# When the decays' maxima and the verdict's ones are issued in a fused decay-attention and gated-MLP kernel

## The chip, the cores and the metric

The kernel runs on one core of one Trainium2 chip. The metric is the device time in microseconds of one execution. A profiled execution gives a span (first to last recorded instruction) and a trace of every engine: TensorE (PE, with its weight loads as PEld), VectorE (DVE), ScalarE (ACT), GpSimd (POOL) and SyncE (SP), which issues all the DMAs here.

## The reference, cut to what matters

```
for t in range(S):                       # S = 768, 4 batches x 8 heads, D = 40
    y[:, :, t] = r_t @ state
    Sa = state @ a_t
    state = state * w_t - outer(Sa, b_t) + outer(v_t, k_t)
x = y as [batch, 768, 320]
h = gelu(x @ w_in)                       # 320 -> 1024; u, v are its halves
v_n = (v - mean) / sqrt(var + 1e-6) * g_ln
v_s = einsum('ts,bsd->btd', w_sg, v_n) + b_sg
out = x + (u * v_s) @ w_out
```

The decays `w` (named `seq_w` in the kernel) are inputs, so the kernel also has to find out whether its chunked form of the recurrence is safe for them. It takes the maximum of the absolute decays and compares it with 1, and it compares the chunks' products of decays with a least value. If either fails, a plain step-by-step version runs instead.

## The kernel before, in words

The **first part** (`attention`) runs the recurrence in chunks of 64 steps and writes x to DRAM. The first weights of the MLP, the first batch's x and three of its v products are worked into its last stretch. The **second part** (`Mlp.run`, line 980 and on) is a list `seq` of 109 products, numbered from 0, each of which is a group of 8 to 18 matmuls into one PSUM bank:

- `v` (one 128-row tile of v, 8 matmuls of 512 columns), followed on ACT, DVE and POOL by gelu, batch statistics, normalising and a split into a high and a low part, `vh` and `vl`;
- `u` (8 matmuls of 384 columns), followed by gelu;
- `s` (the product along the sequence, 18 matmuls of 384 columns that read `vh` and `vl` of all six v tiles), followed by two DVE operations into `g`, then `gy` on ACT and `gx` on POOL;
- `o` (the output product, 8 or 12 matmuls that read `gy` and `gx`), followed by the residual sum `y` on DVE and a store.

Products 0 to 10 finish u and v of batch 0. Then come 28 products for each of the batches 0, 1 and 2 (11 to 38, 39 to 66, 67 to 94) in the order `SEQ`: s1 s2 s0 s3 s4 v0 s5 v1 o0 o1 o2 s6 s7 v2 u0 v3 u1 v4 v5 o3 o5 o4 u2 u3 u4 u5 u7 u6, where s and o belong to the batch, u and v to the next one. The last 14 are s and o of batch 3. The PSUM banks are taken in turn, eight of them.

Every engine works its own queue in program order (class `InOrder`). Program order comes from two tables. A **job** is a pair (product number, function) and is issued just before that product; of jobs with one number, the one entered first goes first. What follows a product is given to `later` as (lag, rank, function). `tick`, called after each product's matmuls, issues whatever is due, sorted by rank. So a step of lag 2 is issued after the matmuls of the product two further on.

What the change and the prediction's steps touch:

- `GROWTH = 12` (line 31) is the product number of the first of 20 jobs `growth(j)`, entered for the products 12 to 31. `growth` takes one of the five buffers `ws` (which first held pieces of the sequence weights), issues a 192 KB DMA of decays on SP, and enters with lag 2 and rank 8 one DVE reduction of 128 x 384 to a column of `wm`. So the reductions come behind the products 14 to 33.
- Before the s products of the next batch, jobs load x: `load_x(b + 1, n)` for both halves n (eight DMAs on SP) at the batch's first product (11, 39, 67), `split_x` one product later (ACT copies to `xh`, DVE writes `xl`). The v products of the next batch read these.
- `verdict` (line 584) is called as a job at the product 73. It compares `wm` and the decays' products with their limits and reduces each to one column of `fl`. Its inner function `last` is entered with lag 8 and rank 9, so it is issued behind u0, the product 81. `last` clears the column `ends` to ones on DVE, multiplies it with `fl` on TensorE into a bank `fp`, and makes the flag from that on DVE.
- Ahead of `last` in that same tick stand, by rank, DVE operations that the products v2 (80) and u0 (81) entered: gelu's steps (rank 6 and 6.5), `bn_stats` (7) and `bn_aggr` (8) of v2.

```
jobs += [(GROWTH + j, lambda j=j: self.growth(j)) for j in range(20)]
jobs.append((p + 6, lambda: self.later((8, 9, verdict(self.wm)))))
```

The DVE queue therefore holds, behind v2 and u0: gelu of both, the statistics of v2, the clearing of `ends`, and then the flag's operations. TensorE's queue holds: v2, u0, the two passes of `fp`, v3.

Of the kernel before, what the change touches and what calls it, by code (L numbers as in the profile page):

```python
# [9 lines left out]
F32 = mybir.dt.float32  # L10
# [17 lines left out]
GROWTH_MAX = 1.0  # L28
DECAY_MIN = 1e-08
DECAY_LOW = 1e-09  # L30
GROWTH = 12
HI_MIN = float(np.uint32(896 << 20).view(np.float32))
HI_MAX = float(np.uint32(1151 << 20).view(np.float32))
FIRST = 0
# [85 lines left out]
def engines(tc):  # L120
    nc = tc.nc
    return tuple(InOrder(tc, e) for e in (nc.vector, nc.scalar, nc.gpsimd, nc.tensor, nc.sync))
# [6 lines left out]
def attention(tc, a, xd, flag, keep, ps, mlp=None):  # L129
# [3 lines left out]
    V, A, G, T, Q = engines(tc)  # L133
# [450 lines left out]
    def verdict(wm):  # L584

        cf = call.rearrange("p i q -> p (i q)")
        fl = keep.tile([128, 2], F32, name="fl")
        V.tensor_scalar(out=wm, in0=wm, scalar1=GROWTH_MAX, scalar2=None, op0=ALU.is_le)
        V.tensor_scalar(out=cf, in0=cf, scalar1=DECAY_MIN, scalar2=None, op0=ALU.is_ge)
        V.tensor_reduce(out=fl[:, 0:1], in_=wm, axis=mybir.AxisListType.X, op=ALU.min)  # L590
        V.tensor_reduce(out=fl[:, 1:2], in_=cf, axis=mybir.AxisListType.X, op=ALU.min)

        def last():
            ends = keep.tile([128, 1], F32, name="ends")
            V.memset(ends, 1.0)
            fp = ps("fp")
            T.matmul(fp[0:1, 0:2], lhsT=ends, rhs=fl, start=True, stop=True)
            V.tensor_reduce(out=fl[0:1, 0:1], in_=fp[0:1, 0:2], axis=mybir.AxisListType.X, op=ALU.add)
            V.tensor_scalar(out=flag, in0=fl[0:1, 0:1], scalar1=255.5, scalar2=None, op0=ALU.is_lt)

        return last
# [4 lines left out]
class Mlp:  # L606
# [323 lines left out]
    def run(self, ahead, verdict=None):  # L930
# [18 lines left out]
        for b in range(B):  # L949
# [5 lines left out]
            if b == 2 and verdict:  # L955
                jobs += [(GROWTH + j, lambda j=j: self.growth(j)) for j in range(20)]
                jobs.append((p + 6, lambda: self.later((8, 9, verdict(self.wm)))))
# [133 lines left out]
```

## Time and profile before

| | before |
|---|---|
| time, median of 3 runs | 670.6 us (669.77 to 670.92) |
| the profiled execution's own time | 667.9 us |
| its span | 666.2 us |
| PE busy | 580.6 us (87% of the span) |
| DVE busy | 519.8 us (78%) |
| ACT busy | 369.8 us (56%) |
| POOL busy | 385.3 us (58%) |
| mean granted clock of TensorE | 0.899 of full speed |

The profiled execution lies 1.7 us above its own span and 2.7 us below the median of the runs. In the trace an instruction has a start and a length; an idle time in square brackets is that of its engine just before it, with what ended it. All the recorded operations carry one line (L115, the helper that keeps program order), so they are told apart by the names of their tiles. The granted clock is 1.00 at 2.4 GHz and 0.50 at 1.2 GHz.

### The profile page before, as it was taken

How to read it: one execution, taken by the hardware profiler on the slowest of the kernel's cores; microseconds unless marked ns; L12 is line 12 of the kernel's file. 1: busy time of each engine (PE TensorE's matmuls, PEld its weight loads, DVE VectorE, ACT ScalarE, POOL GpSimd, SP SyncE). 2: the span in 40 equal slices, each digit the busy share in tenths (PEclk: the TensorE clock that was granted, in tenths of full speed). 3: DMA queues.
4: the chain of work that ended last, by engine and by line, in shares of the span. 5: the costliest groups of instructions: out<-in, count | busy, mean ns of one | idle time of the engine just before them, and what ended most of it. 6: DMA issues, size and time to landing. Idle time of an engine off the chain costs nothing.

```text
span 666.2 us, 22344 instructions
## 1 busy us (share of the span) xinstructions
PE 580.6 (87%) x8950; PEld 526.7 (79%) x8950; DVE 519.8 (78%) x1118; ACT 369.8 (56%) x1010; POOL 385.3 (58%) x868
## 2 busy tenths in 40 slices
PE   6547999989989899899979864969999999989995
PEld 5436788878878788787878754959999999979994
DVE  7875788989889899897786688887898669666732
ACT  3454587876968769687755644652345245223410
POOL 6588887787877878778872464453332332332321
PEclk8555599999999999999967695969999999999999
DMA  6723233444434534333435240451422003000001
GB/s 222 231 80 79 80 94 107 117 120 107 110 102 115 122 109 108 103 89 94 104 94 145 81 130 22 126 156 49 125 66 84 31 0 102 1 30 13 19 30 37
DMA packets 60498, 60.49 MB, mean 91 GB/s; under 512 B 36256, under 2 KB 50336, under 8 KB 60384
## 3 DMA queue, kind: packets, MB, share of 16 engines
q1 hardware_dynamic: 60384, 58.96, 31.4%
q8 instruction: 73, 1.20, 0.8%
q14 instruction: 41, 0.34, 0.2%
HBM read 51.07 MB, written 7.86 MB: 88 GB/s over the span
## 4 chain that ended last, share of the span: by engine, by line
PE 54%; DVE 25%; ACT 12%; issue 6%; DMA 3%; POOL 1%; SPq 0%; POOLq 0%; DVEq 0%; ACTq 0%
PE sg L115 15%; PE hu L115 7%; PE op L115 6%; PE hv L115 6%; PE ru L115 4%; PE ab L115 4%; DVE at L115 3%; PE pq L115 3%; DVE fixed L115 3%; DVE n L115 2%; PE sp L115 2%; PE yp L115 2%; DVE ex L115 2%; ACT xt L115 2%; ACT nts L115 2%
## 5 line engine op out<-in xcount | busy, mean ns | idle before, releaser
L115 POOL TENSOR_TENSOR tg<-x,n 128x126 f32<-128x126 f32 (+21 forms) x348 | 127.9, 368 | 42.8 <-DVE n L115 10.5
L115 POOL TENSOR_TENSOR x<-x,tg 128x126 f32<-128x126 f32 (+21 forms) x348 | 133.4, 383 | 27.3
L115 POOL TENSOR_TENSOR gx<-g,gy 128x384 fp32r<-128x384 f32 x32 | 33.3, 1045 | 84.9 <-ACT gy L115 84.9
L115 PE MATMUL sg<-wsh,vh 128*128 128x384 f32 x192 | 66.4, 346 | 5.0 <-ACT vh L115 5.0
L115 ACT ACTIVATE nts<-ab 32x256 f32<-32x256 f32 x192 | 62.0, 323 | 11.0 <-DVE at L115 8.6
L115 PE MATMUL sg<-wsh,vl 128*128 128x384 f32 x192 | 66.1, 344 | 1.5 <-POOL vl L115 1.5
L115 PE MATMUL yp<-pqs,kbt 128*64 128x64 f32 x768 | 49.9, 236 | 18.9 <-DVE pqs L115 15.4
L115 PE MATMUL sg<-wsl,vh 128*128 128x384 f32 x192 | 65.8, 343 | 0.0
L115 PE MATMUL ab<-at,kb 64*64 64x64 f32 x1536 | 41.9, 248 | 25.7 <-DVE kb L115 18.9
L115 PEld LDWEIGHTS ab<-at,kb 64*64 64x64 f32 x1536 | 35.1, 155 | 33.7 <-issue 18.3
L115 PE MATMUL pq<-rt,vut 128*128 128x128 f32 x384 | 59.8, 304 | 1.7 <-DVE yt L115 1.6
L115 PEld LDWEIGHTS yp<-pqs,kbt 128*64 128x64 f32 x768 | 40.5, 147 | 22.1 <-DVE pqs L115 16.0
L115 ACT CAST gy<-g 128x384 fp32r<-128x384 f32 x32 | 16.4, 513 | 74.3 <-DVE g L115 74.3
L115 PEld LDWEIGHTS pq<-rt,vut 128*128 128x128 f32 x384 | 51.6, 208 | 4.8 <-DVE yt L115 2.5
L115 ACT COPY vs<-sc 64x160 f32<-64x160 f32 x88 | 28.3, 321 | 44.0 <-DVE sc L115 43.1
L115 POOL TENSOR_TENSOR vl<-v,vh 128x512 fp32r<-128x512 f32 x24 | 31.3, 1305 | 26.6 <-ACT vh L115 26.6
L115 ACT CAST vh<-v 128x512 fp32r<-128x512 f32 x24 | 14.9, 620 | 57.2 <-DVE v L115 57.2
L115 PE MATMUL yp<-rt,s 80*40 80x64 f32 x704 | 46.2, 232 | 0.0
L115 DVE SCALAR_TENSOR_TENSOR g<-sg,gl,bt 128x384 f32<-128x384 f32 x32 | 19.7, 615 | 30.0 <-PE sg L115 28.1
L115 POOL TENSOR_TENSOR rs<-rs,mhalf 128x1 f32<-128x1 f32 x24 | 13.4, 560 | 50.6 <-DVE rs L115 43.7
L115 PEld LDWEIGHTS sg<-wsh,vh 128*128 128x128 f32 x192 | 36.8, 192 | 5.8 <-ACT vh L115 5.7
L115 DVE TENSOR_TENSOR at<-ab,mask 64x256 f32<-64x256 f32 x96 | 35.8, 408 | 6.1 <-PE ab L115 5.4
(134 smaller groups left out, 1639.3 us busy)
## 6 DMA issues: line engine op xcount, KB each, us to landing
main<-main SPq DMA_DIRECT2D x88, 160.8 KB
vu<-vs SPq DMA_DIRECT2D x24, 160.0 KB
vs<-vb SPq DMA_DIRECT2D x24, 160.0 KB
rt<-rt SPq DMA_DIRECT2D x48, 80.0 KB
vut<-vt SPq DMA_DIRECT2D x24, 160.0 KB
xd<-yt SPq DMA_DIRECT2D x96, 40.0 KB
ws<-seq_w SPq DMA_DIRECT2D x20, 192.0 KB
xt<-xd SPq DMA_DIRECT2D x16, 192.0 KB
```

Of the source, the lines that this page charges most:

```text
L115: return self.tc.keep_in_program_order(f(*a, **k))
```

## The change

The 20 jobs `growth` begin at the product 34, so their loads are issued ahead of the products 34 to 53 and their reductions behind the products 36 to 55. The tile `ends` is taken and cleared at the head of `verdict`, at the product 73, instead of in `last`.

```diff
-GROWTH = 12
+GROWTH = 34
...
         fl = keep.tile([128, 2], F32, name="fl")
+        ends = keep.tile([128, 1], F32, name="ends")
+        V.memset(ends, 1.0)
         V.tensor_scalar(out=wm, in0=wm, scalar1=GROWTH_MAX, scalar2=None, op0=ALU.is_le)
         V.tensor_scalar(out=cf, in0=cf, scalar1=DECAY_MIN, scalar2=None, op0=ALU.is_ge)
         V.tensor_reduce(out=fl[:, 0:1], in_=wm, axis=mybir.AxisListType.X, op=ALU.min)
         V.tensor_reduce(out=fl[:, 1:2], in_=cf, axis=mybir.AxisListType.X, op=ALU.min)
 
         def last():
-            ends = keep.tile([128, 1], F32, name="ends")
-            V.memset(ends, 1.0)
             fp = ps("fp")
             T.matmul(fp[0:1, 0:2], lhsT=ends, rhs=fl, start=True, stop=True)
```

## Rows read from the trace of the kernel before

**Rows 1.** The page, its part 2: granted clock in 40 slices of 16.7 us.

```profile
PEclk8555599999999999999967695969999999999999
```

**Rows 2.** Waits of PE, 413 to 666 us: total us, times, longest.

```profile
PE sg L115 <- ACT vh L115: 5.0, 2, 3.8
PE fp L115 <- DVE ends L115: 2.8, 1, 2.8
PE sg L115 <- POOL vl L115: 1.5, 2, 1.1
PE op L115 <- ACT gy L115: 0.8, 1, 0.8
PE op L115 <- POOL gx L115: 0.5, 1, 0.5
```

**Rows 3.** Timeline: an s product's last wait; then 592 to 600 us.

```profile
441.95 0.69 PE L115 MATMUL sg<-wsh,vl 128*128 128x384 f32 x1 [0.34 <-POOL vl L115]
...
592.87 0.86 PE L115 MATMUL hv<-wih,xh 128*128 128x512 f32 x3
...
595.77 0.51 PE L115 MATMUL hu<-xl,wih 128*128 128x384 f32 x2
...
598.87 0.18 DVE L115 BATCH_NORM_AGGREGATE mv<-bs 128x2 f32<-128x6 f32 x1
599.00 0.06 DVE L115 MEMSET ends<- 128x1 f32 x1
...
599.11 0.19 PE L115 MATMUL fp<-fl,ends 128*1 128x2 f32 x2 [2.83 <-DVE ends L115]
...
599.23 1.47 PE L115 MATMUL hv<-wih,xh 128*128 128x512 f32 x3
```

**Rows 4.** Stretches around the wait: us, PE, PEld, DVE, ACT, POOL busy, clock, DMA.

```profile
598.00:600.00 2.00, 0.89 (x4) 0.72 (x5) 1.33 (x7) 0.00 (x0) 0.20 (x1) 0.87 0.00 0
600.00:602.00 2.00, 2.00 (x6) 1.56 (x5) 0.00 (x0) 0.00 (x0) 0.35 (x1) 0.50 0.00 0
```

**Rows 5.** Timeline, PE: v2, v3, then s1, batch 1; s1 of batch 3.

```profile
534.16 0.86 PE L115 MATMUL hv<-wih,xh 128*128 128x512 f32 x3
...
537.40 0.86 PE L115 MATMUL hv<-wih,xh 128*128 128x512 f32 x3
...
558.26 0.34 PE L115 MATMUL sg<-wsh,vh 128*128 128x384 f32 x1
...
621.74 0.34 PE L115 MATMUL sg<-wsh,vh 128*128 128x384 f32 x1
```

**Rows 6.** Timeline, DVE, 576.5 to 579 us: the verdict's last reduction.

```profile
577.79 0.35 DVE L115 TENSOR_REDUCE fl<-call 128x1 f32<-128x192 f32 x1
```

**Rows 7.** Tile ws: ns min/median/max, first and last start.

```profile
L115 SPq DMA_DIRECT2D ws<-seq_w x20: 327/346/572, 444.4 to 493.7; - x20
L115 DVE TENSOR_REDUCE wm<-ws x20: 534/542/548, 455.7 to 499.8; 128x1 f32<-128x384 f32 x20
```

**Rows 8.** Timeline, DVE: y of o4 in batch 0, g of s1, end of split_x; y of o4, batch 1.

```profile
498.43 0.54 DVE L115 TENSOR_TENSOR y<-op,xt 128x384 f32<-128x384 f32 x1
...
504.92 0.60 DVE L115 SCALAR_TENSOR_TENSOR g<-sg,gl,bt 128x384 f32<-128x384 f32 x1
...
510.32 0.56 DVE L115 TENSOR_TENSOR xh<-xt,xh 64x384 fp32r<-64x384 f32 x1
...
555.26 0.54 DVE L115 TENSOR_TENSOR y<-op,xt 128x384 f32<-128x384 f32 x1
```

**Rows 9.** Timeline, PE: s1 (39) and v0 (44) behind the loads of batch 2's x.

```profile
499.55 0.34 PE L115 MATMUL sg<-wsh,vh 128*128 128x384 f32 x1
...
515.39 0.86 PE L115 MATMUL hv<-wih,xh 128*128 128x512 f32 x3
```

**Rows 10.** Timeline, SP: the issues of batch 2's x.

```profile
499.39 4.38 SPq L115 DMA_DIRECT2D xt<-xd  x8
```

**Rows 11.** A stretch of batch 1's loads: us, DVE busy, clock, DMA share, GB/s.

```profile
443.00:445.00 2.00, 1.97 (x5) 0.50 0.85 250
```

## The prediction, made before the change was run

> **What bounds the kernel now.** I began with the clock by slices. Its last low digit is the slice from 433 to 450 us, behind the start of the second part at about 413 us; from there on it is 9 in every slice [rows 1]. A slice of 16.7 us can hide a short stop, so the next view was the waits of PE from 413 us to the end. There are only five kinds: two for the splits of v, four waits of which the last ends at 441.95 us [rows 3]; two for `gy` and `gx` of the last products; and between them one single wait of 2.8 us, of `fp` for `ends` [rows 2]. So the second part is bound by TensorE, and another engine's work matters there only if it makes TensorE wait. The timeline around that wait shows why. u0's last matmuls end at 595.77 + 0.51 = 596.28 us. DVE then still works on gelu of v2 and u0 and on the statistics of v2, and clears `ends` only at 599.00 us, behind `bn_stats` and `bn_aggr`. `fp` runs at 599.11 us after 2.83 us of idling, and v3, which needs nothing of the verdict, stands behind it until 599.23 us [rows 3]. After that the granted clock is 0.50, that is 1.2 GHz, through 600 to 602 us, and the mean of the two microseconds before is 0.87: it fell after the idle stretch [rows 4].
>
> **Part 1, the ones.** What `fp` still needs after the change is `fl`, and its last reduction begins at 577.79 us and takes 0.35 us [rows 6]: 18 us early. The ones are cleared just before that. So TensorE goes from u0 through `fp` to v3 at once. The price of the wait can be read against a control: batch 1 runs the same order of products without a verdict. From the start of v2 to the start of s1 of the next batch takes
>
> - batch 1: 558.26 - 534.16 = 24.10 us, and batch 2: 621.74 - 592.87 = 28.87 us, a difference of 4.77 us [rows 3, 5];
> - of these, v2 to v3: 3.24 against 6.36 us, so 3.12 us lie in the idle stretch and `fp` itself;
> - and v3 to s1: 20.86 against 22.51 us, so 1.65 us are matmuls at half the clock.
>
> The two passes of `fp` stay: from 599.11 to 599.23 us, 0.12 us. The gain is 4.77 - 0.12 = **4.65 us**, of which 3.0 us are the wait and 1.65 us the clock. The clearing of 0.06 us [rows 3] moves to the product 73 on a DVE that TensorE does not wait for there; if that cover were gone it would cost those 0.06 us and no more. What is late next: v3, u1, v4, v5 come 3 us earlier on DVE's queue, which had idled meanwhile. In batch 1 the same products follow u0 without a gap and PE waits for none of them [rows 2, 5], so I set nothing against it. The flag itself is read by the branch behind the last product, long after.
>
> Here one thing is not sure. The row shows the clock falling after this idle stretch in this one execution. The Trainium skill, in "TensorE: Matmul & The Clock Gate" (Part 1: The HAM clock gate), says that the monitor runs freely and does not restart with the kernel, so that the point of a change of clock differs between runs of one kernel. By the trace the sum is 4.65 us; by that rule some executions of the kernel before would not lose the 1.65 us, and the sum would be 3.0 us. No row here shows an execution of that kind.
>
> **Part 2, the maxima.** Twenty reductions of 0.54 us, 10.8 us of DVE, leave the stretch from 455.7 to 499.8 us [rows 7], and twenty DMA issues of 0.35 us leave SP there. PE does not wait between 442 us and `fp` [rows 2, 3], so taking them away there gains nothing. They come back behind the products 36 to 55, some 500 to 544 us.
>
> What they could cost there lies between nothing and 10.8 us, if all of it lay on TensorE's path. I take nothing. Behind the products 25 to 33 (u0, the v products, the o products and u2 of batch 0's stretch, where DVE has most to do) nine of them stood, and PE waited for none. After the change that heavy passage of batch 1 holds only four of them (52 to 55) and batch 0's none. In between, the reductions behind 36 to 43 meet the u products and `split_x` of batch 2. Up to the product 55 DVE has always done fewer of them than before, so by the sum of its work it is nowhere later in this stretch than it was; one s product after another then gives it slack. Below nothing I see no room: a gain needs a wait that is not there.
>
> SP is the other queue. The first five loads are now issued ahead of batch 2's x, where before x came straight behind the last stores. Five issues cost 5 x 0.35 = 1.7 us and bring 0.96 MB, which at the 250 GB/s that the DMAs moved in a busy stretch [rows 11] is 3.8 us. But without reductions `y` of o4, whose store stands ahead of these loads, comes earlier: it begins 499.55 - 498.43 = 1.12 us before s1 in batch 0, with reductions, and 558.26 - 555.26 = 3.00 us before s1 in batch 1, without [rows 5, 8, 9]. These 1.9 us pay for the five issues. So SP should start x's loads near 499.4 us as now [rows 10], and x may land up to 3.8 us later, more likely 1 to 2. The split of x ends at 510.88 us and v0, the first to read it, starts at 515.39 us [rows 8, 9]: 4.5 us of slack. Cost nothing. The later loads wait for a buffer that the reduction five places earlier frees, three products before, and the stores of `y` pass between them as they do now in batch 0.
>
> **Sum.** 4.65 us off the profiled execution's 667.9 us gives 663.25 us. The median of the runs is 2.7 us higher, 670.6 us; I carry the difference over: **666.0 us**.
>
> **Rivals.**
>
> *The clock did not fall in the timed runs.* Then the change gives back only the wait and its restart, 3.0 us: 667.6 us. For it speaks that one execution shows one fall; against it that the other long idle stretch, near 433 us, was followed by a slow clock too [rows 1]. Chance 0.28.
>
> *Another wait takes over at `fp`.* If `fp` had also been held by its bank or by something that came last unseen, TensorE would stand until about the same point: 670.6 us, no change. Against it: `fp` started 0.05 us after the clearing ended, `fl` was long done [rows 3, 6], and its bank is that of a product eight places back. Chance 0.07.
>
> *Slower: v0 of batch 2's stretch waits for x.* The place is the product 44, behind `split_x`. If five loads ahead of x hold it up by more than the 4.5 us of slack, TensorE idles for the rest, and 1.65 us more once the clock falls. To be over 1.34 us slower than before (0.2%, about what a measurement of this kernel can tell from no change), it must eat 4.65 + 1.34 = 6.0 us, 4.35 of them idle: x would have to land 8.9 us later than now, against 3.8 us by rows 11. At that point the time is 672 us. Against it also: DVE's `g` of s1 begins 5.4 us after that product's start in batch 0 [rows 8, 9] and hurts nobody, so lateness here has room. Chance 0.07.
>
> **How the numbers follow.** The forecast, wait and clock both given back, has the remaining 0.58. Faster by over 0.2% is this case and the first rival, 0.86; within 0.2% is the second, 0.07; slower the third, 0.07. The range reaches from 664.7 us, the forecast less the spread of 0.6 us above and below the median shown and a little of the difference in clock between runs, to 668.2 us, the first rival with the same spread. It leaves out the two last cases, 0.14, and little of the rest.
>
> **What would show it.** Right: PE's waits after 442 us have no row for `ends`; v3 starts within 0.3 us of u0's end; the clock stays at 1.00 from 450 us to the last products; v2 to s1 of batch 3 takes 24.2 us, as in batch 1; the reductions run from about 501 to 544 us and DVE does not idle for a load in front of them. Wrong: an idle stretch of PE in front of v0 near 515 us, or in front of s1 near 558 us, with the clock falling behind it; or `fp` still waiting, for another name.

## The result, and the profile after

The changed kernel takes 666.94 us (median of 5 runs, 665.09 to 667.71); the kernel before, on the same chip, 670.24 us (669.70 to 670.92). The ratio is 0.9943 with a 95% interval of 0.9923 to 0.9962, which on 670.24 us is 2.5 to 5.2 us less. The ratios in this document are not those of the two medians: they weigh all the runs, save two of the 35 runs of the kernel before in experiments 1 to 4, which lay over 1.5% above its fastest. The forecast was 666.0 us and 4.65 us less.

The waits of TensorE from 413 us to the end, in the profile after (us in total, times, longest):

```profile
PE sg L115 <- ACT vh L115: 4.8, 2, 3.6
PE sg L115 <- POOL vl L115: 1.5, 2, 1.1
PE op L115 <- ACT gy L115: 0.8, 1, 0.8
PE op L115 <- POOL gx L115: 0.5, 1, 0.5
```

This is the list of [rows 2] without the row of `ends` (the first row is 0.2 us shorter); no new row has come. The timeline of TensorE, after (start, length, operation), from v2 to the first s product of batch 3:

```profile
595.14 0.86 PE L115 MATMUL hv<-wih,xh 128*128 128x512 f32 x3
...
598.04 0.51 PE L115 MATMUL hu<-xl,wih 128*128 128x384 f32 x2
598.48 0.19 PE L115 MATMUL fp<-fl,ends 128*1 128x2 f32 x2
598.60 0.96 PE L115 MATMUL hv<-wih,xh 128*128 128x512 f32 x3
...
619.54 0.34 PE L115 MATMUL sg<-wsh,vh 128*128 128x384 f32 x1
```

u0 ends at 598.04 + 0.51 = 598.55 us and `fp` is already under way: nothing stands between. From v2 to v3 takes 598.60 - 595.14 = 3.46 us (before 6.36) and from v3 to s1 20.94 us (before 22.51). The stretch is 24.40 us long instead of 28.87, so it gives **4.47 us**. The clock stays up in it, by stretches of 2 us (PE busy, clock, DMA share, GB/s):

```profile
598.00:600.00 2.00, 2.00 (x12) 1.00 0.00 0
600.00:602.00 2.00, 2.00 (x13) 1.00 0.00 0
```

where [rows 4] had 0.87 and 0.50. The maxima, after (ns min/median/max, first and last start):

```profile
L115 SPq DMA_DIRECT2D ws<-seq_w x20: 328/373/2039, 499.8 to 537.6; - x20
L115 DVE TENSOR_REDUCE wm<-ws x20: 533/544/550, 503.4 to 547.6; 128x1 f32<-128x384 f32 x20
```

The reductions moved by 48 us with their length unchanged [rows 7]. The issues of the loads moved by 44 to 55 us; their median is 0.37 us instead of 0.35, the longest 2.04 us instead of 0.57.

The spans differ by only 666.2 - 663.5 = 2.7 us, less than the 4.47. The other view that one needs is where the second part begins, that is the first matmul of product 0. Before and after:

```profile
412.58 1.33 PE L115 MATMUL hu<-xh,wih 128*128 128x384 f32 x3
```

```profile
414.50 1.33 PE L115 MATMUL hu<-xh,wih 128*128 128x384 f32 x3
```

The first part took 1.9 us more in the profiled execution after. From there to the end it is 666.2 - 412.58 = 253.6 us before and 663.5 - 414.50 = 249.0 us after. This **second part** is what the experiments compare, beside the times.

### The profile page after: what moved, and what is told of

It is laid out like the page before. It is cut to its first block, busy times and chain, and to the rows that moved or that the text cites. A ratio compares the mean times of both kernels' runs of the same rounds, so it can differ in the third digit from the quotient of the medians.

```text
span 663.5 us, 22348 instructions
## 1 busy us (share of the span) xinstructions
PE 577.5 (87%) x8950; PEld 524.3 (79%) x8950; DVE 521.1 (79%) x1118; ACT 369.9 (56%) x1010; POOL 386.6 (58%) x868
## 4 chain that ended last, share of the span: by engine, by line
PE 51%; DVE 26%; ACT 11%; issue 6%; DMA 3%; POOL 1%; SPq 1%; DVEq 0%; POOLq 0%; ACTq 0%
PE sg L115 15%; PE op L115 7%; PE hv L115 6%; PE hu L115 5%; PE ru L115 4%; DVE at L115 4%; PE ab L115 4%; PE pq L115 3%; DVE fixed L115 3%; DVE n L115 2%; PE yp L115 2%; DVE ex L115 2%; ACT xt L115 2%; PE sp L115 2%; PE xp L115 2%
```

## The experiments

Theory A: the wait for the ones, with the slow clock behind it, is the whole gain; moving the maxima costs and gives nothing. Rivals: the maxima give a part (B), cost a part (C), or the change delays the first part (D). All kernels of the first four ran on one chip, against 35 runs of the kernel before with a median of 670.52 us; the next four on another, against 20 runs with 669.09 us.

**1. The ones alone.** `GROWTH` stays at 12.

```diff
-GROWTH = 34
+GROWTH = 12
```

> The ones are cleared at the head of the verdict, the maxima stay at the twelfth product. I call second part the stretch from the first matmul of product 0 to the end of the span: 666.2 - 412.6 = 253.6 us before, 663.5 - 414.5 = 249.0 us after. Theory A (the wait for the ones and its slow clock are the whole gain, the maxima cost and give nothing): second part 249.0 us within 0.3, no wait of TensorE for the ones, time 3 to 5 us under the kernel before. Theory B (moving the maxima gives part of the gain): second part at least 0.5 us longer than 249.0. Theory C (moving the maxima costs something that the changed kernel hides in its gain): second part at least 0.5 us shorter than 249.0.

Measured: 664.21 us, ratio 0.9926 (0.9901 to 0.9952). TensorE, with a span of 662.5 us:

```profile
413.21 1.33 PE L115 MATMUL hu<-xh,wih 128*128 128x384 f32 x3
...
594.05 0.86 PE L115 MATMUL hv<-wih,xh 128*128 128x512 f32 x3
...
618.45 0.34 PE L115 MATMUL sg<-wsh,vh 128*128 128x384 f32 x1
```

Second part 249.3 us, v2 to s1 24.40 us. This is the changed kernel's gain within 0.3 us without its second half. Theory A.

**2. The maxima alone.** The ones are cleared in `last()` as before.

```diff
-GROWTH = 12
+GROWTH = 34
```

> The maxima begin at the product 34, the ones are cleared in last() as before. Theory A: second part 253.6 us within 0.3 where the clock falls behind the wait, 252.0 us where it doesn't; TensorE still waits 2.8 us for the ones; time within 1 us of the kernel before. Theory B: second part shorter than 252.0 us with the wait still there. Theory C: longer than 254.1 us, with a new wait of TensorE behind the products 36 to 60. A fourth possibility, D: the move changes the first part (its end at 412.6 us before, 414.5 us after): then this kernel's first part is near 414.5 us and that of the ones alone near 412.6 us.

Measured: 669.37 us, ratio 0.9999 (0.9972 to 1.0027). TensorE, with a span of 668.1 us:

```profile
414.23 1.33 PE L115 MATMUL hu<-xh,wih 128*128 128x384 f32 x3
...
594.75 0.86 PE L115 MATMUL hv<-wih,xh 128*128 128x512 f32 x3
...
600.99 0.19 PE L115 MATMUL fp<-fl,ends 128*1 128x2 f32 x2 [2.83 <-DVE ends L115]
601.11 1.35 PE L115 MATMUL hv<-wih,xh 128*128 128x512 f32 x3
...
623.62 0.34 PE L115 MATMUL sg<-wsh,vh 128*128 128x384 f32 x1
```

The wait is there to the hundredth, v2 to s1 takes 28.87 us as before, and the second part is 253.9 us. The move of 20 reductions and 20 loads does nothing that these views can show. TensorE from 450 to 550 us, where the reductions stand before (455.7 to 499.8 us) as well as after (503.4 to 547.6), in the kernel before and in the changed kernel (length, PE busy, clock, DMA share, GB/s):

```profile
450.00:550.00 100.00, 100.00 (x542) 1.00 0.20 59
```

```profile
450.00:550.00 100.00, 100.00 (x542) 1.00 0.22 67
```

TensorE is busy throughout in both, at full clock and with the same number of matmuls, so there was no wait for the maxima to make or to take away. By the times alone the move may still be worth up to 0.3% either way. B and C fall as far as the second part shows them. D predicted a late first part for this kernel (414.2 us fits) and an early one for the ones alone (413.2 us, between the two).

**3. The changed kernel again**, unchanged, for the first part.

> The changed kernel once more, for the first part. In its profile the second part began 1.9 us later than before, which hides 1.9 of 4.6 us. Theory A: that is chance, the second part is 249.0 us again within 0.3, and the start of the second part falls anywhere between 412 and 415 us whatever the kernel. Theory D: the change itself delays the first part, and it starts near 414.5 us again.

Measured: 665.83 us, ratio 0.9943 (0.9919 to 0.9968). TensorE, with a span of 661.8 us:

```profile
412.53 1.33 PE L115 MATMUL hu<-xh,wih 128*128 128x384 f32 x3
```

The same program starts its second part at 412.53 us here and at 414.50 us in its first profile; second part 249.3 us. So D falls: the 1.9 us belong to the execution. Over all ten profiles of this case the second part began between 411.8 us (the filled wait below) and 414.7 us (the ones on another queue).

**4. The wait filled with work.** Before the verdict's product, 16 matmuls into the same bank, whose result it overwrites.

```diff
             fp = ps("fp")
+            for _ in range(16):
+                T.matmul(fp[:, 0:384], lhsT=mlp.wih[:, 0, 0:128], rhs=mlp.xh[:, 0, 0:384], start=True, stop=True)
             T.matmul(fp[0:1, 0:2], lhsT=ends, rhs=fl, start=True, stop=True)
```

> As the kernel before, but 16 matmuls of 384 columns into the bank fp stand ahead of the verdict's own, 16 x 0.176 = 2.8 us of work whose result is overwritten. TensorE then works where it waited for the ones, and v3 can start no earlier than before. If 1.65 us of the loss are the slow clock behind the idle stretch: v3 starts 6.4 us after v2 as before, the clock stays at 1.00 behind it, v3 to s1 takes 20.9 us instead of 22.5, second part 251.9 us, time 1 to 2 us under the kernel before. If the slow stretch has another cause (DVE and ACT being late behind the wait): v3 to s1 stays near 22.5 us and the second part near 253.6 us.

Measured: 667.41 us, ratio 0.9978 (0.9952 to 1.0004), on 670.52 us between 3.2 us less and 0.3 us more. TensorE, with a span of 662.7 us:

```profile
411.77 1.33 PE L115 MATMUL hu<-xh,wih 128*128 128x384 f32 x3
...
591.43 0.86 PE L115 MATMUL hv<-wih,xh 128*128 128x512 f32 x3
...
594.67 2.94 PE L115 MATMUL fp<-xh,wih 128*128 128x384 f32 x16
...
597.79 0.96 PE L115 MATMUL hv<-wih,xh 128*128 128x512 f32 x3
...
618.74 0.34 PE L115 MATMUL sg<-wsh,vh 128*128 128x384 f32 x1
```

v3 starts 6.36 us after v2, exactly as late as before, and still the stretch behind it takes 20.95 us instead of 22.51. So 1.56 us of the loss came from the clock that fell after the idle stretch, and not from DVE or ACT being late. The second part is 250.9 us, 1.0 us shorter than expected; that further microsecond lies outside the stretch from v2 to s1: 0.6 us ahead of v2 (591.43 - 411.77 = 179.66 us against 592.87 - 412.58 = 180.29) and 0.5 us behind s1 (43.96 us to the end against 44.46), where the edit changes nothing. The part ahead of v2 can be followed in the trace: the slow clock near 440 us was shorter in this execution. TensorE from 434 to 449 us, the kernel before and this one:

```profile
434.00:449.00 15.00, 9.76 (x35) 0.66 0.57 168
```

```profile
434.00:449.00 15.00, 10.06 (x43) 0.77 0.57 170
```

A mean of 0.66 in 15 us is some 10 us at half clock, 0.77 some 7 us. Whether the 16 matmuls kept the clock up behind `fp`, or whether it would have stayed up in this execution without them, is not shown; the 1.56 us are the price of the slow clock either way. The times alone don't settle this one: their interval reaches past 1.

**5. All twenty maxima in a burst**, at the product 36.

```diff
-jobs += [(GROWTH + j, lambda j=j: self.growth(j)) for j in range(20)]
+jobs += [(36, lambda j=j: self.growth(j)) for j in range(20)]
```

> As the changed kernel, but all twenty maxima are entered at the product 36, ahead of batch 2's x on SP's queue; their reductions stand together behind the product 38, ahead of the split of x on DVE's. There are five buffers, so each load past the fifth waits for a reduction and each reduction for a load. Theory A (the maxima are free only as long as x's split keeps its 4.5 us of slack before v0): the twenty take some 16 us on DVE, x comes behind them, TensorE waits 5 to 12 us at v0 (product 44), the clock falls behind that, second part 256 to 263 us against 249.0 to 249.3 of the changed kernel. Rival (DVE and SP have so much room in this stretch that order doesn't matter): second part within 1 us of 249.2.

Measured: 675.41 us, ratio 1.0085 (1.0055 to 1.0116): slower than the kernel before, although the ones are out of the way. The waits of PE from 445 to 600 us, and TensorE by stretches of 2 us:

```profile
PE hv L115 <- ACT xh L115: 4.4, 1, 4.4
PE hv L115 <- DVE xh L115: 0.9, 1, 0.9
```

```profile
518.00:520.00 2.00, 0.00 (x0) 0.81 0.94 287
520.00:522.00 2.00, 0.60 (x2) 0.50 0.85 273
522.00:524.00 2.00, 1.08 (x3) 0.50 0.03 8
524.00:526.00 2.00, 2.00 (x6) 0.50 0.00 0
```

SP's and DVE's timelines in this kernel say why:

```profile
499.00 16.54 SPq L115 DMA_DIRECT2D ws<-seq_w  x20
515.59 4.34 SPq L115 DMA_DIRECT2D xt<-xd  x8
```

```profile
521.38 1.52 DVE L115 TENSOR_TENSOR xl<-xt,xh 128x384 fp32r<-128x384 f32 x2 [0.53 <-ACT xh L115]
```

The loads hold SP for 16.5 us, x of batch 2 is issued only behind them, and v0 waits for its split, 5.3 us in two pieces. Then TensorE runs at 1.2 GHz from 520 us for the rest of the stretch shown. This is the place that the prediction's third rival named. The second part is 673.8 - 413.66 = 260.1 us, 10.9 us more than the changed kernel's 249.3 in (3). Of these, 9.0 us lie ahead of v2 (603.39 - 413.66 = 189.73 us against 593.25 - 412.53 = 180.72): 5.3 us are the wait, and some 3.7 us are left for the slow clock. The other 1.9 us lie behind s1 (46.0 against 44.2 us), where the last `y` waits 1.9 us for a store that takes 3.8 us, as in experiment 7.

**6. The ones on another queue.** Same place in the program, other engine.

```diff
         def last():
             ends = keep.tile([128, 1], F32, name="ends")
-            V.memset(ends, 1.0)
+            G.memset(ends, 1.0)
```

> As the kernel before, with one edit: the ones are cleared at the same place of the program, in last(), but by GpSimd instead of VectorE. GpSimd's queue is empty from 596.0 us to 599.8 us there. Theory A (what TensorE waited for is the place in DVE's queue, behind the statistics of v2, not the clearing itself): no wait, v2 to s1 24.4 us, second part 249.2 us, time as with the ones alone, ratio to the kernel before 0.990 to 0.996. Rival (any clearing issued so late holds TensorE): TensorE still waits 1 us or more at fp.

Measured: 665.19 us, ratio 0.9942 (0.9919 to 0.9965). GpSimd and TensorE, span 663.1 us:

```profile
597.19 1.01 POOL L115 TENSOR_TENSOR gx<-g,gy 128x384 fp32r<-128x384 f32 x1 [2.13 <-ACT gy L115]
598.14 0.10 POOL L115 MEMSET ends<- 128x1 f32 x1
```

```profile
598.00 0.51 PE L115 MATMUL hu<-xl,wih 128*128 128x384 f32 x2
598.44 0.19 PE L115 MATMUL fp<-fl,ends 128*1 128x2 f32 x2
```

The ones come at 598.24 us, behind GpSimd's `gx` and as u0 is ending, and nothing waits. The clearing takes even longer here (0.10 against 0.06 us). What cost 2.83 us was its place in DVE's queue. The stretch from v2 to s1 is 619.50 - 595.10 = 24.40 us, as in the other kernels without the wait. The second part is 663.1 - 414.65 = 248.5 us, 0.7 us shorter than the 249.2 expected; the difference lies outside that stretch, in parts that the edit doesn't touch.

**7. Two maxima per product**, from 36 to 45.

```diff
-jobs += [(GROWTH + j, lambda j=j: self.growth(j)) for j in range(20)]
+jobs += [(36 + j // 2, lambda j=j: self.growth(j)) for j in range(20)]
```

> As the changed kernel, but two maxima per product, entered from the product 36 to 45, with reductions behind 38 to 47: six loads stand ahead of batch 2's x instead of five, and DVE has ten reductions more before the product 47. Theory A: the slack of 4.5 us holds this, no wait of TensorE near 517 us, second part 249.2 us within 0.3. Rival (the slack is used up already by the change as made): TensorE waits at v0 by 0.5 us or more, second part 249.7 us or longer.

Measured: 665.28 us, ratio 0.9939 (0.9918 to 0.9960). TensorE doesn't wait near v0. DVE's last step of the split, and v0 on TensorE:

```profile
514.57 0.56 DVE L115 TENSOR_TENSOR xh<-xt,xh 64x384 fp32r<-64x384 f32 x1 [0.68 <-ACT xh L115]
```

```profile
517.68 0.86 PE L115 MATMUL hv<-wih,xh 128*128 128x512 f32 x3
```

The split ends 2.55 us before v0; in the changed kernel it ends at 512.10 + 0.56 = 512.66 and v0 starts at 517.66 us, 5.0 us:

```profile
502.45 4.57 SPq L115 DMA_DIRECT2D xt<-xd  x8
...
512.10 0.56 DVE L115 TENSOR_TENSOR xh<-xt,xh 64x384 fp32r<-64x384 f32 x1
...
517.66 0.86 PE L115 MATMUL hv<-wih,xh 128*128 128x512 f32 x3
```

So this order uses half the slack and costs nothing, as expected. But the second part of the profiled execution was 666.3 - 414.02 = 252.3 us, outside the 249.2 expected. The stretch from v2 to s1 is 24.40 us. Most of the rest is at the very end, the chain that ended last (first line) and DVE:

```profile
655.12 5.30 DMA out<-y
```

```profile
660.51 0.56 DVE L115 TENSOR_TENSOR y<-op,xt 128x384 f32<-128x384 f32 x1 [3.43 <-DMA out<-y]
```

One of the last stores took 5.3 us in that execution, and the last `y` waits 3.43 us for its buffer. From s1 to the end it is 46.7 us against 44.0 in the first profile of the changed kernel. The median of 12 runs does not show it.

**8. The kernel before again.**

> The kernel before once more, one look. Two profiles with the wait for the ones have shown a slow clock behind it. If the clock falls every time: v3 to s1 is 22.5 us again, second part 253.6 us within 0.3. If it falls only in some executions: v3 to s1 20.9 us and second part 252.0 us. The start of the second part falls between 411.5 and 415 us.

Measured: 668.61 us. TensorE, with a span of 666.8 us:

```profile
413.55 1.33 PE L115 MATMUL hu<-xh,wih 128*128 128x384 f32 x3
...
600.07 0.19 PE L115 MATMUL fp<-fl,ends 128*1 128x2 f32 x2 [2.83 <-DVE ends L115]
600.19 1.46 PE L115 MATMUL hv<-wih,xh 128*128 128x512 f32 x3
...
622.70 0.34 PE L115 MATMUL sg<-wsh,vh 128*128 128x384 f32 x1
```

v3 to s1 is 22.51 us again, second part 253.3 us. In all three profiles with the wait the clock fell behind it, and v3 to s1 took the same 22.51 us. In stretches of 0.2 us (PE busy, clock, DMA share, GB/s) the fall can be placed; the kernel before, the maxima alone (2), and this one:

```profile
599.40:599.60 0.20, 0.20 (x1) 0.69 0.00 0
```

```profile
601.40:601.60 0.20, 0.20 (x2) 0.71 0.00 0
```

```profile
600.40:600.60 0.20, 0.20 (x2) 0.61 0.00 0
```

A mean of 0.69 in 0.2 us is 0.076 us at full and 0.124 us at half clock, so it fell at 599.48 us; the other two give 601.48 and 600.44 us. v3 started at 599.23, 601.11 and 600.19 us: the fall came 0.25, 0.37 and 0.25 us behind it.

## Why the prediction was right

**The step of the ones** held. TensorE goes from u0 through `fp` to v3, the clock stays up, and the kernel with the ones alone (1) and the one with the clearing on another queue (6) show that it was this wait and this queue. The stretch gave 4.47 us against 4.65 forecast. The difference of 0.18 us has two parts. v2 to v3 takes 3.46 us, 0.22 us more than in batch 1 without a verdict (3.24 us, rows 5), where the prediction left 0.12 us for `fp`, the time between two starts: 0.10 us. v3 to s1 takes 20.94 us where batch 1 had 20.86: 0.08 us. Of the gain, 6.36 - 3.46 = 2.90 us are the wait and 22.51 - 20.94 = 1.57 us the clock; the filled wait (4) separates the two and puts the clock at 1.56 us.

**The step of the maxima** held in the profiled executions: the move alone leaves the second part within 0.3 us of the kernel before, and TensorE is busy throughout from 450 to 550 us with it and without it (2). The times say less. On the first chip the ones alone have a median 1.6 us below the changed kernel (664.21 and 665.83 us, 1 and 3), on the second chip the ones on GpSimd, with the maxima where they were, and the moved maxima of (7) are 0.1 us apart (665.19 and 665.28). A cost of some tenths of a per cent in executions that were not profiled is not ruled out.

The finer reasoning held in the main. The split of x ends 5.0 us before v0, where [rows 8, 9] had 4.5; DVE waited for none of the twenty loads in the changed kernel. The five issues ahead of x took 2.55 us where the prediction had 1.7, and x was issued 517.66 - 502.45 = 15.2 us before v0 instead of 515.39 - 499.39 = 16.0: `y` coming early paid for most of the five issues and not for all, and nothing waited for x. Two small slips changed nothing: from u0 on, the heavy passage of batch 1 holds three of the reductions (53 to 55) and not four, and five loads of 192 KB are 0.98 MB and not 0.96.

**The rivals.** The first, that the clock did not fall in the timed runs, found no support: it fell in three profiles of three, and the time of the ones alone (3.2 to 6.6 us less by its interval on 670.52 us) lies above the 2.90 us of the wait alone. The intervals of the other kernels without the wait (the burst aside) contain both 2.90 and 4.47 us. The rule of the Trainium skill behind it ("TensorE: Matmul & The Clock Gate", Part 1: The HAM clock gate) is that the monitor does not restart with the kernel and the point of a change moves from run to run. In the second part of this kernel it hardly moves against the work: 0.25 to 0.37 us behind v3's start in three executions whose second parts began up to 1.7 us apart (8). The measurement decides for the forecast here, but for these executions only. The three profiles have the fall at nearly one place of the work, so they are not three different tests of that rule; and the filled wait's profile, where the slow clock near 440 us lasted some 7 us and not 10, shows that the clock and the work can stand to each other otherwise. That the clock falls behind this wait in every execution is not shown, why the two keep step in these three is open, and the unprofiled runs don't show their clock stretch by stretch. The second rival is out, `fp` waits for nothing. The third named the right place and the right direction, and the burst (5) shows its price, 9.0 us ahead of v2, but the change as made stays clear of it.

**The number.** 666.94 us was measured and 666.0 forecast. The traces explain 4.47 us of gain, the medians show 3.3 us and the ratio's interval 2.5 to 5.2 us. The difference may come from the first part, whose end moves by almost 3 us between the ten profiles whatever the kernel; the unprofiled runs don't show it. The prediction carried the 2.7 us between its profiled execution and the median over as if that were fixed, and it is of the same size as this movement. A difference of 1 us between medians of five runs is not something the change need do, and that the forecast came so close to the median is in part luck; the 4.47 us of the stretch are not.

## What to carry to other kernels

A constant that TensorE needs late should be made early, or on a queue that has nothing late ahead of it at that time: the 0.06 us clearing cost 4.5 us here, because it stood in DVE's queue behind work that depended on the products just issued. If TensorE is the bound, look in its list of waits for the single ones; a twin of the stretch without the wait (here batch 1) prices it, slow clock included. Work that hides well could be moved about freely here until it stood ahead of a load on a shared queue: there count the slack of whoever reads the load. To compare two executions, go from one fixed instruction to another around the changed place: v2 to s1 was 24.39 or 24.40 us in all six profiles without the wait and with no dummy work, while the rest of the second part moved by tenths of a microsecond to several.

## What the runs showed that was not expected

- The idle stretch of 2.83 us, and the 22.51 us from v3 to s1 behind it, came back to the hundredth in three profiles, while the first part's end moved by almost 3 us between executions.
- A store of 192 KB near the end took 5.3 us in one execution (7), and the last `y` waited 3.4 us for it; in the burst (5) it was 3.8 us and a wait of 1.9 us. Why is open.
- An idle stretch cost more than itself each time: 2.83 us of waiting for the ones came with 1.57 us of slow clock, and in the burst 5.3 us of waiting made the way to v2 9.0 us longer, with the clock at 0.50 behind it.
